# A fused attention and MLP block: two centred tiles, finer loads, new instruction orders

## The chip, the cores and the metric

The kernel runs on one core of one Trainium2 chip. The metric is the device time of one execution in microseconds (us), the median of several executions. A run is called fast when it is near the fastest of its kernel; slow ones are named. "Clock" is the clock granted to TensorE as a share of full speed.

The engines are TensorE (PE; its weight loads are PEld), VectorE (DVE), ScalarE (ACT), GpSimd (POOL) and SyncE (SP), which here only issues DMAs. A *transposing DMA* reads a tile from SBUF and writes it back transposed.

## The reference

```
phi = lambda t: where(t > 0, t + 1, exp(t)) + 1e-6        # 16 heads of 28
q, k, v = split(layernorm(x) @ wqkv)                      # x: 2048 x 448, bf16
kv  = einsum("bhsd,bhse->bhde", phi(k), v)
z   = einsum("bhsd->bhd", phi(k))
o   = einsum("bhqd,bhde->bhqe", phi(q), kv) / (phi(q) . z + 1e-6)
h   = x + o @ wo
n   = layernorm(h)
out = h + (gelu(n @ w_gate) * (n @ w_up)) @ w_down        # 448 -> 1792 -> 448
```

The 2048 rows are 16 tiles of 128. Tile t needs statistics, normalisation and a transpose before TensorE can project it to K and Q (four matmuls of 448 columns each, called K_t and Q_t below).

## The kernel before

Every instruction is a task with a name, an engine, and the buffers it reads and writes. The semaphores follow from the buffers. The order on each engine is a plain list of task numbers, found by a search outside the kernel, so an engine waits for its next task even if a later one could run:

```
ORDERS = ("26 34 32 43 41 63 66 ...", ...)                # one string per engine: PE, ACT, DVE, POOL, SP
```

Loads are issued in this order, all on SP but tile 1:

```
dma_x("sp", 0, 1);  tx1 = dma_x("act", 1, 2)
dma_w3("sp", wqk_sb, 0, 2 * D, b_wqk, "dwqk")             # Q and K weights together, 672 KB
dma_w1("sp", wqk_sb, 0, 2 * D, b_wqk, "dwqk_t")           # their last 64 rows
dma_x("sp", 2, 4); dma_x("sp", 4, 8); dma_x("sp", 8, 12); dma_x("sp", 12, 16)
# ... V weights, output weights
```

The first four tiles are normalised on DVE and transposed on PE, the others on POOL and by a transposing DMA:

```
def ln_tile(t):
    ln_stats(...)                                         # DVE: mean and variance
    ln_rstd_act(...)                                      # ACT: ln, then exp, gives 1/std
    if t < N_PE_TR:                                       # 4
        # DVE: xnn = (x - mean) * rstd                    "normD_t"
        # PE: four 128x128 transposes; ACT and DVE copy half of the result each to xnT
    else:
        # POOL: xnn = (x - mean) * rstd                   "normP_t"
        G.add("sp", lambda e: e.dma_start_transpose(xnT[:, t, :, :], xnn[:, i, :]), ...)   # "xT_t"
```

Later the same pattern returns: the attention output of tiles 2p and 2p+1 is divided by its denominator on DVE ("pn"), transposed by one DMA for the pair ("oT_p") and multiplied on PE ("the output projection of pair p"). V itself is never made: PE sums phi(K) times the normalised x over all tiles, in PSUM (the memory that TensorE writes to), and multiplies the sum by the V weights ("the fold"). TensorE first runs a warm-up of ones times ones, `WARM = 40` matmuls of 128 columns, while nothing else is there to do.

## Time and profile before

| | before |
|---|---|
| time, median of 3 | 194.24 us (194.19 to 194.25) |
| profiled execution: span, clock | 197.8 us, 0.95 (a slow execution) |
| PE, DVE, ACT, POOL busy in it | 98, 67, 39, 26% |
| second profile of the same kernel (first experiment): span, clock | 193.1 us, 1.00 |

### The profile page before, as it was taken

How to read it: one execution, taken by the hardware profiler on the slowest of the kernel's cores; microseconds unless marked ns; L12 is line 12 of the kernel's file. 1: busy time of each engine (PE TensorE's matmuls, PEld its weight loads, DVE VectorE, ACT ScalarE, POOL GpSimd, SP SyncE). 2: the span in 40 equal slices, each digit the busy share in tenths (PEclk: the TensorE clock that was granted, in tenths of full speed). 3: DMA queues.
4: the chain of work that ended last, by engine and by line, in shares of the span. 5: the costliest groups of instructions: out<-in, count | busy, mean ns of one | idle time of the engine just before them, and what ended most of it. 6: DMA issues, size and time to landing. Idle time of an engine off the chain costs nothing.

```text
span 197.8 us, 4145 instructions
## 1 busy us (share of the span) xinstructions
PE 193.7 (98%) x1572; PEld 106.9 (54%) x1572; DVE 132.0 (67%) x355; ACT 78.1 (39%) x226; POOL 50.7 (26%) x92
## 2 busy tenths in 40 slices
PE   7999999999999999999999999999999999999995
PEld 7554555555767776654454445444444454444454
DVE  3899988999999989988786537244445422444412
ACT  3797645599943324141330420023444200334200
POOL 7067710640451955235222024000000000000000
PEclk9999999999999999999999999999999999999999
DMA  6966449994587046420217272600200010100011
GB/s 194 375 174 88 94 96 209 221 215 63 102 291 124 16 50 117 102 53 23 56 26 153 57 56 52 133 21 30 46 0 3 0 46 4 46 0 3 0 46 46
DMA packets 35331, 16.97 MB, mean 86 GB/s; under 512 B 27696, under 2 KB 34032, under 8 KB 35312
## 3 DMA queue, kind: packets, MB, share of 16 engines
q1 hardware_dynamic: 35168, 16.60, 38.4%
q8 instruction: 12, 0.20, 0.4%
q10 hardware_dynamic: 144, 0.11, 0.2%
q14 instruction: 7, 0.06, 0.1%
HBM read 8.26 MB, written 1.84 MB: 51 GB/s over the span
## 4 chain that ended last, share of the span: by engine, by line
PE 90%; DMA 4%; DVE 4%; POOL 1%; issue 0%; DVEq 0%; POOLq 0%
PE ps L603 42%; PE ps L575 22%; PE ps L404 9%; PE ps L523 7%; PE ps L423 5%; PE ps L605 3%; DMA x_sb<-in_A_x_dram 2%; DVE st L348 2%; DMA xnT<-xnn 2%; DVE pk L417 1%; PE ps L471 0%; PE ps L462 0%; POOL wqk_sb L302 0%; PE ps L550 0%; DVE xnn L370 0%; DVE mv L349 0%
## 5 line engine op out<-in xcount | busy, mean ns | idle before, releaser
L605 PE MATMUL ps<-hnT,wgu_sb 64*128 64x512 bf16 (+1 forms) x490 | 89.9, 342 | 0.0
L603 PE MATMUL ps<-hnT,wgu_sb 64*128 64x512 bf16 (+1 forms) x490 | 89.6, 342 | 0.0
L623 ACT ACTIVATE gl<-ps 128x256 bf16<-128x256 f32 x112 | 37.1, 381 | 88.5 <-PE ps L605 86.4
L603 PEld LDWEIGHTS ps<-hnT,wgu_sb 64*128 64x128 bf16 x490 | 46.3, 96 | 35.1 <-issue 3.1
L625 DVE TENSOR_TENSOR hh<-ps,gl 128x256 bf16<-128x256 f32 x112 | 42.5, 416 | 34.0 <-ACT gl L623 33.7
L605 PEld LDWEIGHTS ps<-hnT,wgu_sb 64*128 64x128 bf16 x490 | 45.2, 96 | 3.7 <-DVE hh L625 0.5
L575 PE MATMUL ps<-wd_sb,hh 128*128 128x448 bf16 (+1 forms) x238 | 45.2, 351 | 0.0
L575 PEld LDWEIGHTS ps<-wd_sb,hh 128*128 128x128 bf16 x238 | 23.3, 99 | 21.1 <-issue 1.3
L404 PE MATMUL ps<-wqk_sb,xnT 128*128 128x448 bf16 x128 | 28.2, 362 | 0.1
L488 POOL TENSOR_TENSOR t<-pq,zbc 128x448 f32<-128x448 bf16 x15 | 16.6, 1115 | 33.3 <-DVE pq L484 20.5
L579 DVE TENSOR_TENSOR x_sb<-ps,x_sb 128x448 bf16<-128x448 f32 (+1 forms) x17 | 10.0, 592 | 19.6 <-PE ps L575 19.6
L348 DVE BATCH_NORM_STATS2 st<-x_sb 128x6 f32<-128x448 bf16 x32 | 19.1, 612 | 3.5 <-DMA x_sb<-in_A_x_dram 3.4
L404 PEld LDWEIGHTS ps<-wqk_sb,xnT 128*128 128x128 bf16 x128 | 12.3, 99 | 12.1 <-DMA xnT<-xnn 0.5
L423 PE MATMUL ps<-pk,xnn 128*128 128x448 bf16 x64 | 14.4, 363 | 0.0
L523 PE MATMUL ps<-w,pqnT 112*128 112x448 bf16 x64 | 14.1, 362 | 0.0
L558 POOL TENSOR_SCALAR hn<-x_sb,nm,rs 128x448 bf16<-128x448 bf16 x14 | 10.9, 779 | 8.1 <-DMA hnT<-hn 7.4
L529 DVE TENSOR_TENSOR x_sb<-ps,x_sb 128x448 bf16<-128x448 f32 x16 | 9.5, 617 | 3.8 <-PE ps L523 3.8
L415 ACT ACTIVATE e<-ps 128x448 bf16<-128x448 f32 x16 | 8.7, 541 | 5.4 <-PE ps L404 3.6
L417 DVE SCALAR_TENSOR_TENSOR pk<-ps,e 128x448 bf16<-128x448 f32 x16 | 9.9, 616 | 0.2
L388 POOL TENSOR_SCALAR xnn<-x_sb,nm,rs 128x448 bf16<-128x448 bf16 x12 | 9.0, 749 | 3.5 <-ACT rs L357 3.5
L423 PEld LDWEIGHTS ps<-pk,xnn 128*128 128x128 bf16 x64 | 6.5, 101 | 6.2
L495 DVE TENSOR_TENSOR pqn<-pq,rd 128x448 bf16<-128x448 bf16 x16 | 9.6, 622 | 0.0
(65 smaller groups left out, 125.0 us busy)
## 6 DMA issues: line engine op xcount, KB each, us to landing
out_dram<-x_sb SPq DMA_DIRECT2D x15, 112.0 KB, 1.7
wd_sb<-in_B_w_down_dram SPq DMA_DIRECT2D x1, 1568.0 KB, 7.7
x_sb<-in_A_x_dram SPq DMA_DIRECT2D x3, 448.0 KB, 5.4
wgu_sb<-in_B_w_gate_dram SPq DMA_DIRECT2D x1, 896.0 KB, 11.9
wgu_sb<-in_B_w_up_dram SPq DMA_DIRECT2D x1, 896.0 KB, 16.5
wqk_sb<-in_A_wqkv_dram SPq DMA_DIRECT2D x1, 672.0 KB, 4.8
wgu_sb<-in_B_w_gate_dram SPq DMA_DIRECT2D x1, 672.0 KB, 6.0
wgu_sb<-in_B_w_up_dram SPq DMA_DIRECT2D x1, 672.0 KB, 8.4
```

Source lines behind the costliest of these rows:

```text
L348: op("dve", lambda e: e.bn_stats(st[:, t, :], src_ap), [b_src], [b_st[t]], "bnst%s_%d" % (tag, t))
L404: ins = e.matmul(ps[:, bk, 0:D], xnT[:, t, k, :], wqk_sb[:, k, c0:c0 + D], start=(k == 0), stop=(k == 3))
L417: op("dve", lambda e: e.scalar_tensor_tensor(pk[:, ip, :], psK, EPS, e1[:, i, :], ALU.max, ALU.add), [b_ps[bk], b_e1[i]], [b_pk[ip]], "pk_ ...
L423: ins = e.matmul(ps[:, BK_PT[c], 0:D], xnn[:, t % XN_R, c * 128:(c + 1) * 128], pk[:, ip, :], start=(t == 0), stop=(t == T - 1))
L488: op(eng, lambda e, t=t, n=n: e.tensor_tensor(t1[:, n, :], pq[:, t, :], zbc[:, :], ALU.mult), [b_pq[t]] + b_z, [b_t1[n]], "t1%s_%d" % (eng ...
L523: ins = e.matmul(ps[:, BK_OUT[n], 0:D], pqnT[0:GW, i2, n, g, :], w2[:, g, :], start=(g == 0), stop=(g == NG - 1))
L558: op("pool", lambda e, t=t, sh=sh: e.tensor_scalar(hn[:, sh, 0:D], x_sb[:, t, :], nm2[:, t:t + 1], rs2[:, t:t + 1], ALU.add, ALU.mult), [b ...
L575: ins = e.matmul(psO, hh[:, j, (t % HR) * 128:(t % HR + 1) * 128], wd_sb[:, j, c0:c1], start=(j == 0), stop=(j == NJ - 1))
L603: e.matmul(psG[:, jj * N:(jj + 1) * N], wgu_sb[A_, k, j * 128:(j + 1) * 128], hnT[A_, ka_, c0:c0 + N], start=(k == 0), stop=(k == NK - 1))
L605: ins = e.matmul(psU[:, jj * N:(jj + 1) * N], wgu_sb[B_, k, j * 128:(j + 1) * 128], hnT[B_, kb_, c0:c0 + N], start=(k == 0), stop=(k == NK ...
L623: G.add("act", lambda e, gi=gi, cs_=cs_, psG=psG: e.activation(gl[:, gi, cs_], psG[:, cs_], AF.Gelu_apprx_tanh), r=[b_ps[BK_G[i]]], w=[b_g ...
L625: op("dve", lambda e, dst=dst, srcU=srcU, srcL=srcL: e.tensor_tensor(dst, srcU, srcL, ALU.mult), [b_ps[BK_U[i]], b_glh], [b_ar[j_][t % HR] ...
```

## The change

Its intent is to start the dense matmul work earlier. The first two tiles are only centred before their transpose. Since a row of (x - mean) times the weights only lacks the factor 1/std of that row, that factor is applied as the scale of the activations that read K and Q. Tile 1's statistics move to ACT. Q and K weights and x come in more pieces, K before Q. All loads stay ahead of the transposing DMAs, as before. All five orders are new, over the whole kernel.

```diff
-    WARM = 40
+    CEN = (0, 1);  ACT_ST = (1,);  WARM, WARM2, NW2 = 33, 0, 0
-    SEQ = "Q0 K0 K1 Q1 K2 Q2 ..."
+    SEQ = "K0 K1 Q0 K2 Q1 Q2 ..."
...
-        dma_w3("sp", wqk_sb, 0, 2 * D, b_wqk, "dwqk")
-        dma_w1("sp", wqk_sb, 0, 2 * D, b_wqk, "dwqk_t")
-        dma_x("sp", 2, 4)
-        dma_x("sp", 4, 8)
+        dma_w1("sp", wqk_sb, 0, 2 * D, [None, b_wqt], "dwqk_t")
+        dma_wqk(1);  dma_x("sp", 2, 3);  dma_wqk(0);  dma_x("sp", 3, 4)
+        dma_x("sp", 4, 6);  dma_x("sp", 6, 8)
...
+            if t in ACT_ST:          # sum(x)/D and sum(x*x)/D by two ACT passes with accum_out
+                act_exp(... AF.Identity, scale=1.0 / D, accum_out=mv1[:, t, 0:1] ...)
+                act_exp(... AF.Square, scale=D ** -0.5, accum_out=mv1[:, t, 1:2] ...)
...
+                if t in CEN:         # xc = x - mean
+                    op("dve", lambda e: e.tensor_scalar(xc[...], x_sb[:, t, :], mv1[:, t, 0:1], None, ALU.subtract), ...)
...
+            sc = rs1[:, t:t + 1] if t in CEN else 1.0
+            eks.append(act_exp(lambda e: e.activation(e1[:, i, :], psK, AF.Exp, scale=sc), ...))
+            if t in CEN:             # relu on ACT, then an all-SBUF add on DVE ("pka")
+                act_exp(lambda e: e.activation(pk[:, ip, :], psK, AF.Relu, scale=sc), ...)
...
 ORDERS: every number changed
```

## The prediction

> **What bounds the kernel now.** I read the page from the top: busy shares, forty slices, chain that ended last. Then the timeline of the first 24 us, TensorE's timeline up to 60 us, and the busy time by stretch.
>
> ```profile
> PE 193.7 (98%) x1572; PEld 106.9 (54%) x1572; DVE 132.0 (67%) x355; ACT 78.1 (39%) x226; POOL 50.7 (26%) x92
> ...
> PE 90%; DMA 4%; DVE 4%; POOL 1%; issue 0%; DVEq 0%; POOLq 0%
> ```
>
> TensorE (PE) is busy for 193.7 of 197.8 us, and the last chain is 90% PE. The rest of the chain lies before about 18 us: x loads, statistics, one transposing DMA. So matmul work sets the time, and a change that takes away no matmul can only start the dense part earlier or close holes in it. How much is there? The timeline, PE rows (start, length, operation, idle before):
>
> ```profile
> 1.11 4.30 PE L342 MATMUL ps<-ones_bf 128*128 128x128 bf16 x40 [1.11 <-POOL ones_bf L315]
> 5.37 0.38 PE L378 MATMUL ps<-ident,xnn 128*128 128x128 bf16 x4
> 6.07 0.40 PE L378 MATMUL ps<-ident,xnn 128*128 128x128 bf16 x4 [0.32 <-DVE xnn L370]
> 6.31 3.30 PE L404 MATMUL ps<-wqk_sb,xnT 128*128 128x448 bf16 x16
> 9.45 0.90 PE L378 MATMUL ps<-ident,xnn 128*128 128x128 bf16 x8
> 10.21 1.73 PE L404 MATMUL ps<-wqk_sb,xnT 128*128 128x448 bf16 x8
> ```
>
> The 4.3 us of ones times ones is warm-up, not work. Real projections start at 6.31. A projection's four matmuls start 0.79 us apart from the next four (11.78, 12.57), 0.197 each, so sixteen need 3.15: 6.31 to 9.45 is dense. The eight transposes start 0.055 us apart and need 0.45; they take 9.45 to 10.21, so 0.3 is lost, to the normalised tile 3 on VectorE (DVE). One hole follows:
>
> ```profile
> 17.29 0.95 PE L423 MATMUL ps<-pk,xnn 128*128 128x448 bf16 x4
> 18.30 0.96 PE L404 MATMUL ps<-wqk_sb,xnT 128*128 128x448 bf16 x4
> ```
>
> 18.30 should be 18.08: 0.2 lost, put down to a transposing DMA. From there to 60 us I find no hole, only starts at their pitch. What can be won is therefore the delay before 6.31, plus 0.3, plus 0.2.
>
> What sets 6.31? The chain of tile 0:
>
> ```profile
> 3.37 0.63 DVE L348 BATCH_NORM_STATS2 st<-x_sb 128x6 f32<-128x448 bf16 x1 [3.37 <-DMA x_sb<-in_A_x_dram]
> 4.03 0.18 DVE L349 BATCH_NORM_AGGREGATE mv<-st 128x2 f32<-128x6 f32 x1
> 4.24 0.29 ACT L355 ACTIVATE ln<-mv,eps_t 128x1 f32<-128x1 f32 x1 [1.75 <-DVE mv L349]
> 4.57 0.20 ACT L357 ACTIVATE rs<-ln 128x1 f32<-128x1 f32 x1
> 4.85 0.37 DVE L370 TENSOR_SCALAR xnn<-x_sb,mv,rs 128x448 bf16<-128x448 bf16 x1
> 5.79 0.38 ACT L383 ACTIVATE xnT<-ps 128x256 bf16<-128x256 bf16 x1 [0.28 <-PE ps L378]
> 5.92 0.28 DVE L385 COPY xnT<-ps 128x256 bf16<-128x256 bf16 x1
> ```
>
> x lands at 3.37, is normalised at 4.85, and its transpose is in SBUF at 6.20. Two other things end at nearly the same moment: tile 1's transposes, issued ahead of the first projection, at about 6.3, and the QK weights, issued at 1.24 with 4.8 us to landing by the page's list of issues: 1.24 + 4.8 = 6.04. So all three have to move together, which explains why the change is a bundle.
>
> **What the Trainium skill says.** "TensorE: Matmul & The Clock Gate", Part 1, says that the array runs at half rate until it has been busy for a free-running window of about 3.4 us, with the transition near 4 us. The trace agrees: warm-up weight loads last 152 ns and drop to 98 at about 5.1, 4.0 after 1.11. "DMA: Bandwidth & Descriptors", "Anatomy of one DMA", says that the fixed cost of a transfer is mostly the write receipt; in this trace a 112 KB piece of x takes 2.6 us, one of twice the size 4.3 behind the weights, so what is queued ahead counts as much as size. "ScalarE: Activation LUTs", "What ACT_TABLE_LOAD costs", says that a per-partition operand in place of an immediate adds about 93 ns to an activation. Rows with such a bias (0.29) and without (0.20) agree. "VectorE: DVE Perf Modes", "Why PSUM operands drop a tier", says that a PSUM operand costs a perf mode; here the PSUM combine takes 0.616 and an all-SBUF bf16 add 0.381.
>
> **The change part by part.**
> *Centring.* Tiles 0 and 1 are transposed as x minus mean; 1/std is applied per row as the scale of the activations that read K and Q. That is exact, since rows of x become rows of the product. Off tile 0's path: from 4.21 (mean ready) to 4.85, 0.6 us. Centring starts at 4.25, ends at 4.62; the path from 4.85 to 6.20 took 1.35, so the same steps end at 5.60.
> *Statistics of tile 1 on ScalarE (ACT).* Two passes of 448 (I take 0.54, as L432; an estimate, from SBUF) from 3.5 to 4.6 replace 0.63 + 0.18 on DVE. But ACT also evicts half of tile 0: after these passes come tile 0's ln (0.29) and exp (0.20) and tile 1's ln (0.29), so that eviction starts at about 5.4 and ends near 5.8. So the first projection starts at about 5.85, not 5.65.
> *Weights.* Ahead of K now stand x0, x1, the 112 KB tail and K itself, 0.67 MB, in place of about 1.0 MB. Bytes by time (busy time by stretch: 221 GB/s in 2 to 3 us, 335, 405) reach 0.67 MB at about 4.3; today's 1.0 MB is reached at 5.1 and lands at 6.04, 0.9 later. So K lands near 5.2 to 5.6, in time for 5.85. Q, 0.45 MB later, lands near 6.5 and is wanted at 5.85 + 8 x 0.197 = 7.4: hidden. x2 should land near 5.5 and x3 near 6.7, where both landed at 6.74.
> *Warm-up.* 33 matmuls instead of 40 at 0.107 us: it ends near 4.65, when the first transposes can come. It costs nothing if the clock still rises at about 5.1.
> *Work added and moved.* ACT: two statistics passes and two relus of K, some 2 us, less nothing. DVE: one bn pair (0.8) and two PSUM combines (1.2) go, two adds (0.76) and two small memsets come; about 1 us less. POOL: two more normalisations (1.4) and two memsets fewer (1.3).
> *Tiles 2 and 3.* The orders are plain lists of numbers that I decoded by counting operations in the diff. PE runs K0, K1, Q0, transposes of 2, Q1, transposes of 3, K2. Twelve matmuls from 5.85 end at 8.2, Q1 near 9.2. Tile 2's statistics start after the evictions, at 5.9, and it is normalised near 7.6: in time. Tile 3's rsqrt stands in ACT's order after K0's relu and exp, K1's exp, two ln and an eviction: about 9.2, and its DVE normalisation ends near 9.7. So transposes of tile 3 wait about 0.5, and K2 starts near 9.9 to 10.0 instead of 10.21.
>
> Sum: 0.46 earlier at the start, 0.2 more lost at tile 3 (0.5 against 0.3), 0.2 gained if the hole at 18.3 closes, as the transposing DMAs start some 1.3 us earlier. Net 0.46 - 0.2 + 0.2, about **0.45 us**. The ceiling, with no hole at all, is 0.46 + 0.3 + 0.2, about 1.0. The timed runs may have larger holes than this profile: they last 194.24, the profiled execution 199.48 at a granted clock of 0.95. At a higher clock the matmuls shrink, and the DVE, busy 14.9 of 15 us from 10 to 25, begins to bind; there its relief of about 1 us would be worth more. I choose 0.7.
>
> **Rivals.**
> *Another wait takes the place (order-bound).* ACT becomes the gate: it was busy 4.94 of 5 us from 10 to 15 and gets 2 us more, mostly before 10. If tile 3's rsqrt slips another 0.5, all is given back: 194.2 to 194.5. The two sums on ACT may also need a separate step to read the accumulator, which the trace cannot show. Against it: DVE relief, and an order searched for this.
> *The K weights stay the gate.* Rows of 896 bytes instead of 1792 mean more packets for the same bytes; if K still lands at 6.0 the start gains 0.25 and the total is 194.0. For it: today's landing is only 0.3 before the start.
> *The clock rises late.* With 33 matmuls and thin transposes from 4.7 to 5.9, the window in which the array counts as busy may be missed; the next is 3.4 us away, in which half rate would cost up to 1.7: 195.3. I give it one in ten. Against it: 3.5 us of warm-up are left, and the switch at 5.1 fell in before the old first transpose.
> *All hidden anyway.* DVE bounds the stretch from 10 to 25 us, not PE, so an earlier start ends at the same place: 194.2. Against it: PE is dense there at its own pitch.
>
> **Range and chances.** 194.24 - 0.7 = **193.5 us**. Low end: the whole ceiling and half a us of holes that only timed runs have, 192.7. High end: start gained and given back, 194.4. Two per cent would be 3.9 us, four times the ceiling in this trace: faster 0.02. Slower by 3.9 would need a late clock and a new stall together: 0.02. Within 2%: 0.96.
>
> **What would show it.** In the changed kernel's timeline: centring at 4.25; first projection between 5.6 and 6.0, a K projection not Q; K weights 3.5 to 4 us from issue to landing; tile 2's statistics before 6; tile 3's transposes apart from tile 2's with a wait of about 0.5 before them, ended by DVE and behind it ACT; K2 near 9.95; no hole near 18; from 25 us on the same rows as before, all earlier by one constant. The prediction is wrong if the first projections run 0.37 apart instead of 0.197 (clock), if the start stays at 6.2 (weights), or if the reordered middle between 30 and 60 us shows holes that were not there.

## The result, and the profile after

The changed kernel took **194.82 us** (194.72, 194.83, 194.81, 193.74, 195.02, and one slow run of 196.75 at clock 0.991). The kernel before, on the same chip in the same rounds, took 194.25 (194.16 to 194.46). The ratio is 1.0018, 95% interval 0.9994 to 1.0043. Ratios here and below are the mean time of one kernel's fast runs over that of the other's fast runs of the same rounds, so not quite the ratio of the medians quoted. The time is within 2%, as predicted, but outside the range: 194.82 against a high end of 194.4.

The page of the changed kernel, its busy line and its last chain:

```profile
PE 186.8 (97%) x1565; PEld 110.0 (57%) x1565; DVE 130.7 (68%) x355; ACT 79.3 (41%) x232; POOL 52.4 (27%) x96
...
PE 88%; DMA 6%; DVE 2%; SPq 2%; issue 0%; ACT 0%; DVEq 0%; ACTq 0%
```

DMA has gone from 4 to 6% of the chain. The chain in order of time says where one piece of that is (start, length, what):

```profile
59.63 0.39 ACT gl L667
60.06 4.84 DMA pqnT<-pqn
64.95 1.69 PE ps L567 x8
```

At 65 us, where the prediction saw only matmuls at their pitch, TensorE waits for a transposing DMA that takes 4.84 us. The timeline of the beginning, PE rows of the changed kernel (start, length, operation, idle before):

```profile
1.04 3.70 PE L357 MATMUL ps<-ones_bf 128*128 128x128 bf16 x33 [1.04 <-POOL eps_t L331]
4.57 1.02 PE L412 MATMUL ps<-ident,xc 128*128 128x128 bf16 x8
5.82 2.49 PE L439 MATMUL ps<-wqk_sb,xnT 128*128 128x448 bf16 x12 [0.23 <-DMA wqk_sb<-in_A_wqkv_dram]
8.31 0.28 PE L412 MATMUL ps<-ident,xnn 128*128 128x128 bf16 x2
8.62 0.93 PE L439 MATMUL ps<-wqk_sb,xnT 128*128 128x448 bf16 x4
9.38 0.28 PE L412 MATMUL ps<-ident,xnn 128*128 128x128 bf16 x2
10.77 0.40 PE L412 MATMUL ps<-ident,xnn 128*128 128x128 bf16 x4 [1.11 <-DVE xnn L404]
11.01 0.54 PE L439 MATMUL ps<-wqk_sb,xnT 128*128 128x448 bf16 x2
11.87 2.07 PE L439 MATMUL ps<-wqk_sb,xnT 128*128 128x448 bf16 x10 [0.33 <-DVE xnT L419]
```

The first projection (line 439) starts at 5.82, as planned. Then come two holes: 1.11 us before tile 3's transposes, ended by DVE's normalised tile, and 0.33 us inside K2, ended by DVE's copy of tile 2's second half. The same rows of the kernel before, at full clock:

```profile
6.39 3.19 PE L404 MATMUL ps<-wqk_sb,xnT 128*128 128x448 bf16 x16
9.41 0.39 PE L378 MATMUL ps<-ident,xnn 128*128 128x128 bf16 x4
10.09 0.40 PE L378 MATMUL ps<-ident,xnn 128*128 128x128 bf16 x4 [0.29 <-DVE xnn L370]
10.32 1.68 PE L404 MATMUL ps<-wqk_sb,xnT 128*128 128x448 bf16 x8
```

So the changed kernel is 0.57 us ahead at the first projection and 0.69 behind at K2 (11.01 against 10.32). Why DVE is late there is in its own rows of the changed kernel:

```profile
8.63 0.63 DVE L367 BATCH_NORM_STATS2 st<-x_sb 128x6 f32<-128x448 bf16 x1 [0.38 <-DMA x_sb<-in_A_x_dram]
...
10.35 0.36 DVE L404 TENSOR_SCALAR xnn<-x_sb,mv,rs 128x448 bf16<-128x448 bf16 x1
11.00 0.63 DVE L367 BATCH_NORM_STATS2 st<-x_sb 128x6 f32<-128x448 bf16 x1 [0.28 <-DMA x_sb<-in_A_x_dram]
11.54 0.27 DVE L419 COPY xnT<-ps 128x256 bf16<-128x256 bf16 x1
```

The copy of tile 2's second half (11.54), which K2 needs, stands in DVE's order behind statistics of tile 8 (11.00), which waited for x. Tile 3's normalisation (10.35) is held by ACT, whose rows before it are these:

```profile
7.42 0.62 ACT L454 ACTIVATE pk<-ps,rs 128x448 bf16<-128x448 f32 x1
7.94 1.15 ACT L452 ACTIVATE e<-ps,rs 128x448 bf16<-128x448 f32 x2
9.37 0.48 ACT L374 ACTIVATE ln<-mv,eps_t 128x1 f32<-128x1 f32 x2 [0.28 <-DVE mv L368]
9.76 0.36 ACT L417 ACTIVATE xnT<-ps 128x256 bf16<-128x256 bf16 x1
10.03 0.28 ACT L376 ACTIVATE rs<-ln 128x1 f32<-128x1 f32 x2
```

Tile 3's 1/std is made at 10.03. The two `ln` before it are those of tiles 3 and 5 and waited for DVE, whose statistics of tile 5 waited for x until 8.63.

Starts of some matmul groups, read from the two traces at full clock:

| | before | changed | changed minus before |
|---|---|---|---|
| first projection | 6.39 | 5.82 | -0.57 |
| K2 | 10.32 | 11.01 | +0.69 |
| the fold of K and V (all tiles' K done) | 38.61 | 39.14 | +0.53 |
| last tile group's last down projection | 185.16 | 184.97 | -0.19 |
| span | 193.1 | 192.9 | -0.2 |

One profiled execution each cannot show the 0.57 us between the medians, for executions of one kernel differ by one microsecond and more. But it shows the shape: the front loses 1.1 us against its start, and the later part, with its new orders, is shorter by 0.7 in spite of the stall at 65 us. The size of the front's loss differs from execution to execution: this one of the kernel before took 194.83, 0.6 over its median, with a stall of its own at 15.91 (below), and in a_mid, whose first 50 us are those of the changed kernel, the fold starts at 38.38.

### The profile page after: what moved, and what is told of

It is laid out like the page before. It is cut to its first block, busy times and chain, and to the rows that moved or that the text cites. A ratio compares the mean times of both kernels' runs of the same rounds, so it can differ in the third digit from the quotient of the medians.

```text
span 192.9 us, 4146 instructions
## 1 busy us (share of the span) xinstructions
PE 186.8 (97%) x1565; PEld 110.0 (57%) x1565; DVE 130.7 (68%) x355; ACT 79.3 (41%) x232; POOL 52.4 (27%) x96
## 3 DMA queue, kind: packets, MB, share of 16 engines
HBM read 8.26 MB, written 1.84 MB: 52 GB/s over the span
## 4 chain that ended last, share of the span: by engine, by line
PE 88%; DMA 6%; DVE 2%; SPq 2%; issue 0%; ACT 0%; DVEq 0%; ACTq 0%
PE ps L647 35%; PE ps L619 22%; PE ps L439 10%; PE ps L649 7%; PE ps L567 7%; PE ps L465 6%; DMA x_sb<-in_A_x_dram 3%; DMA pqnT<-pqn 3%; SPq L290 2%; DVE st L367 1%; PE ps L515 0%; DVE pk L456 0%; PE ps L506 0%; PE ps L594 0%; PE ps L548 0%
## 5 line engine op out<-in xcount | busy, mean ns | idle before, releaser
L649 PE MATMUL ps<-hnT,wgu_sb 64*128 64x512 bf16 (+1 forms) x490 | 86.2, 334 | 0.0
L647 PE MATMUL ps<-hnT,wgu_sb 64*128 64x512 bf16 (+1 forms) x490 | 86.0, 333 | 0.0
L669 DVE TENSOR_TENSOR hh<-ps,gl 128x256 bf16<-128x256 f32 x112 | 42.7, 419 | 32.5 <-ACT gl L667 32.2
L647 PEld LDWEIGHTS ps<-hnT,wgu_sb 64*128 64x128 bf16 x490 | 45.5, 94 | 24.9 <-issue 2.2
L649 PEld LDWEIGHTS ps<-hnT,wgu_sb 64*128 64x128 bf16 x490 | 42.5, 94 | 5.7 <-DVE hh L669 3.3
L619 PE MATMUL ps<-wd_sb,hh 128*128 128x448 bf16 (+1 forms) x238 | 43.4, 341 | 0.0
L439 PE MATMUL ps<-wqk_sb,xnT 128*128 128x448 bf16 x128 | 27.2, 353 | 0.6 <-DVE xnT L419 0.3
L465 PE MATMUL ps<-pk,xnn 128*128 128x448 bf16 x64 | 13.8, 353 | 0.1
L422 POOL TENSOR_SCALAR xnn<-x_sb,nm,rs 128x448 bf16<-128x448 bf16 x14 | 10.4, 749 | 4.0 <-ACT rs L376 3.8
L371 POOL TENSOR_SCALAR nm<-mv 128x1 f32<-128x1 f32 (+1 forms) x21 | 4.8, 236 | 24.0 <-DVE mv L368 23.4
L452 ACT ACTIVATE e<-ps 128x448 bf16<-128x448 f32 x14 | 7.6, 546 | 6.9 <-PE ps L439 5.4
L567 PEld LDWEIGHTS ps<-w,pqnT 112*128 112x128 bf16 x64 | 5.6, 98 | 7.5 <-DMA pqnT<-pqn 1.1
```

The lines of the kernel that those rows point to most:

```text
L422: op("pool", lambda e: e.tensor_scalar(xnn[:, i, 0:D], x_sb[:, t, :], nm1[:, t:t + 1], rs1[:, t:t + 1], ALU.add, ALU.mult), [b_x[t], b_nm1 ...
L439: ins = e.matmul(ps[:, bk, 0:D], xnT[:, t, k, :], wqk_sb[:, k, c0:c0 + D], start=(k == 0), stop=(k == 3))
L465: ins = e.matmul(ps[:, BK_PT[c], 0:D], xnn[:, t % XN_R, c * 128:(c + 1) * 128], pk[:, ip, :], start=(t == 0), stop=(t == T - 1))
L567: ins = e.matmul(ps[:, BK_OUT[n], 0:D], pqnT[0:GW, i2, n, g, :], w2[:, g, :], start=(g == 0), stop=(g == NG - 1))
L619: ins = e.matmul(psO, hh[:, j, (t % HR) * 128:(t % HR + 1) * 128], wd_sb[:, j, c0:c1], start=(j == 0), stop=(j == NJ - 1))
L647: e.matmul(psG[:, jj * N:(jj + 1) * N], wgu_sb[A_, k, j * 128:(j + 1) * 128], hnT[A_, ka_, c0:c0 + N], start=(k == 0), stop=(k == NK - 1))
```

## The experiments

Fifteen runs, all correct: the kernel before again, and fourteen edited kernels. The first two calls ran on one chip, the third and the fourth on two others, so kernels of different calls are best compared by their ratios to before. Medians leave out slow runs; the changed kernel's is over all six (194.81 without the slow one). "Before" in each line is the kernel before in the same rounds. Where a line says stall, it is the start-to-start distance of two matmuls less their normal pitch (columns at 2.4 per nanosecond plus 2.5 ns), read from the records of the trace; it is a little longer than the idle time that a page row shows.

| experiment | us, median (range) | ratio to before, 95% |
|---|---|---|
| changed kernel | 194.82 (193.74 to 195.02) | 1.0018 (0.9994 to 1.0043) |
| a_front: tile 3 first | 196.0 (195.41 to 196.46) | 1.0090 (1.0072 to 1.0108) |
| a_load: loads as before | 194.95 (194.2 to 195.93) | 1.0039 (1.0013 to 1.0065) |
| a_mid: orders of before from 50 us on | 195.35 (194.2 to 195.89), one slow 199.18 left out | 1.0047 (1.0018 to 1.0077) |
| a_delay: 10 more warm-up matmuls | 196.77 (195.14 to 197.18) | 1.0094 (1.0056 to 1.0131) |
| a_oT: pair 3's row repaired | 194.16 (193.11 to 194.73) | 0.9973 (0.9941 to 1.0006) |
| a_front2: tile 3 first, ACT too | 197.65 (196.26 to 199.19) | 1.0165 (1.0112 to 1.0218) |
| b_late: front of before, repaired late orders | 193.78 (193.47 to 194.4) | 0.9968 (0.9943 to 0.9993) |
| a_shift: warm-up of fewer instructions | 193.27 (192.75 to 194.19) | 0.9948 (0.9920 to 0.9976) |
| a_swap68: tiles 6 and 8 swapped | 194.06 (193.72 to 195.51) | 0.9992 (0.9962 to 1.0023) |
| a_best: swap and repair | 194.03 (193.25 to 194.91) | 0.9977 (0.9943 to 1.0011) |
| b_late_shift | 193.94 (193.71 to 194.56) | 0.9978 (0.9956 to 1.0001) |
| **a_swap_shift: swap and fewer instructions** | **193.0 (192.72 to 193.58)** | **0.9928 (0.9905 to 0.9951)** |
| a_all: swap, repair, fewer instructions | 193.33 (192.9 to 193.41), one slow 280.58 left out | 0.9938 (0.9916 to 0.9959) |
| b_shift: before with fewer instructions | 194.5 (193.74 to 195.0) | 1.0001 (0.9976 to 1.0025) |

### First call: front, loads, late orders

**b_again** is the kernel before without an edit, for a profile at full clock.

> The kernel before once more, for a profile at the full clock, since its first profile fell in a slow execution at a granted clock of 0.95. The dense matmul part of the changed kernel, 5.82 to 190.6 us less its stalls of some 3.5, is about 181.3 us. If the kernel before, at full clock, starts its projections at 6.3 and ends near 190.1, it must have some 2.5 us of stalls of its own that the slow profile (0.5 us in the first 20 us) did not show: I expect 2 to 3 us of stalls, or else a granted clock below 1.0 in its ordinary runs.

It took 194.83 in its one execution, at clock 1.00, and is the comparison used above. Its stalls after the first projection add up to 2.4 us, as expected. One thing in it corrects my reading: the fold starts at 38.61 where the slow profile had 38.76, although the clock was 1.00 against 0.95. Were this stretch made of matmuls at their pitch, it would have been some 1.3 us shorter (32.5 us from first projection to fold, times 1 - 0.189/0.197, the starts of matmuls in the two profiles). The difference is nearly all one hole: K4 waits 1.04 us at 15.91 here, while in the slow profile it starts at its pitch (14.93). So "PE is dense there at its own pitch" was true of one slow profile and not of this one. What makes the hole comes with b_shift.

**a_front** puts tile 3's statistics and normalisation, and tile 2's second half of transposes ("tr1_2"), ahead of other work:

```diff
 PE:  ... q_0 tr0_2
-q_1 tr1_2
+tr1_2 q_1
 DVE: ... normD_2
-bnst_5 bnag_3 bnag_5 ck_0 bnst_4 ck_1 bnag_4 normD_3 bnst_8 evxD_2
+bnag_3 ck_0 evxD_2 normD_3 bnst_5 bnag_5 bnst_4 bnag_4 evxD_3 ck_1
 ACT: ... rk_0 ek_0
-ek_1 ln_3 ln_5 evxA_2 rs_3 rs_5 rk_1 ln_4 eq_0
+ln_3 rs_3 evxA_2 ek_1 ln_5 rs_5 evxA_3 rk_1 ln_4 eq_0
```

> The changed kernel with only the orders of the first 12 us altered: tile 3's aggregate, rsqrt and normalise, and tile 2's evictions, go ahead of the statistics of tiles 5, 4 and 8 that wait for late x pieces. Theory ORDER (the in-order VectorE queue puts work that waits for late x pieces ahead of tile 3): the waits of 1.28 us and 0.49 us before tile 3's transposes and K2 fall to under 0.4 together, and the time falls by 1.2 to 1.6 us, to about 193.2. Theory LOADS (the loads as a whole end too late, 15.3 us, and the transposing DMAs land behind them at 15.8): the same waits vanish but come back before K5 at 14 to 16 us; the time falls by at most 0.4, to 194.3.

K2 started at 9.98, close to what I had predicted for the change. It did not help: the bill moved. PE rows of this run:

```profile
9.98 0.92 PE L439 MATMUL ps<-wqk_sb,xnT 128*128 128x448 bf16 x4
11.86 0.93 PE L439 MATMUL ps<-wqk_sb,xnT 128*128 128x448 bf16 x4 [0.96 <-ACT pk L454]
13.36 0.93 PE L439 MATMUL ps<-wqk_sb,xnT 128*128 128x448 bf16 x4 [0.57 <-ACT pq L476]
```

After K2 the next projection waits 0.96 us for ACT's relu of K1 to free its PSUM bank, and the one after that 0.57 us for ACT again. By K4 the 1.03 us gained at K2 are gone (17.16 against 17.10 in the changed kernel). So in this stretch ACT has no room: what is done sooner for tile 3 is done later for the tiles before. That the kernel took 196.0, over a microsecond more than the changed one, has another reason in its trace: K6 waits 1.09 us, at 20.51, for a transposing DMA of 3.86 us. What slows such DMAs is found further down.

**a_load** gives the changed kernel the load list of before (Q and K weights whole, x in pieces of 1, 1, 2, 4, 4, 4 tiles):

```diff
-dwqk_t dwk dx2 dwq dx3 dx4 dx6 dx8 ...
+dwqk dwqk_t dx2 dx4 dx8 ...
```

> The changed kernel with only the loads of before: Q and K weights in one transfer ahead of their tail, x in pieces of 2 and 4 tiles. First projection near 6.1 instead of 5.82. Theory LOADS: tiles 4 to 7 land near 7.9 and 8 to 11 near 9.0 instead of 8.6 and 11.0, so statistics 5 and 8 no longer hold tile 3; stalls before K2 fall from 1.8 to about 0.6; all loads end near 12.7 instead of 15.3; time 193.6 to 193.9. Theory ORDER alone: the order of ScalarE and VectorE keeps tile 3 late whatever lands; time 194.5 or more.

The first projection started at 6.19, just after the weights landed (6.15), and K2 at 11.73, both later than in the changed kernel. In the traces with the finer loads and the short warm-up the first projection starts between 5.77 and 6.14, so the finer loads bring it forward by 0.05 to 0.4 us. The time, 194.95, is within the spread of the changed kernel's, and the fold starts only 0.10 later (39.24). That is not because K2 does not matter: this trace lacks two breaks after K2 (0.49 and 0.28 us) that the changed kernel's has. In all eight traces with the changed kernel's TensorE order that have no such break (this one, a_mid, a_delay, a_oT, a_shift, a_swap68, a_best, a_swap_shift), K4 starts 5.57 or 5.58 us after K2, so what is lost at K2 is lost.

**a_mid** keeps the changed kernel to about 50 us and takes the old orders from there.

> The changed kernel up to about 50 us, then the orders of before on every engine (and the warm-up pow of GpSimd ahead of the first products with z instead of among them). The stall of 0.99 us at 64.95 before the third output projection should vanish if the new orders of the second half caused it: time down by 0.7 to 1.0, to about 193.7. If instead it comes from matmuls being faster at full clock than the engines that feed them, the old orders stall there as well and the time stays at 194.6.

The stall at 65 us was gone from its trace and still it took 195.35. Going back to the old late orders is no repair.

### Second call: the start itself, the stall, the late orders alone

**a_delay** runs the warm-up longer:

```diff
-    WARM, WARM2, NW2 = 33, 0, 0
+    WARM, WARM2, NW2 = 43, 0, 0
```

> The changed kernel with 43 warm-up matmuls instead of 33, nothing else: it takes the early start away again, the first projection moves from about 5.9 to about 6.4 us. Theory START (the prediction's: the first projection sets when the dense part ends): the time rises by 0.4 to 0.6 us over the changed kernel. Rival (the start is not on the path; K2 waits for tile 3 behind late x pieces and ScalarE, whatever the start): it rises by 0.15 or less. A late rise of the clock would show as first projections 0.37 us apart in the short warm-up and not here.

The first projection came at 6.59, 0.77 later, but K2 at 11.12, only 0.11 later: the start is off the path. Yet it took 196.77, two us more (1.5 by the ratios). The trace has three stalls on transposing DMAs: 1.39 us before K6, 1.12 at 56.6 and 1.10 at 67.0. Ten more warm-up matmuls did something to DMAs 50 us later. That was the clue for the third call.

**a_oT** repairs what I took for the cause of the stall at 65 us. In POOL's order a power (0.58 us) and the denominators of tile 7 stood ahead of those of tile 6, which is wanted first:

```diff
 POOL: mhalf t1p_1 ... t1p_5
-t1p_7 powwarm t1p_6
+t1p_6 t1p_7          # powwarm right after mhalf
 DVE:  dr_6 rd_6 pn_6 moved ahead;  ACT: deA_6 moved ahead
```

> The changed kernel with one local repair in the middle: the warm-up pow of GpSimd and the product for tile 7 no longer stand ahead of the product for tile 6, and tile 6's reduction, reciprocal and normalisation go earlier on VectorE and ScalarE, so that the transposing DMA for tiles 6 and 7 is issued near 57.5 us instead of 60.06. Expected: the wait of 0.99 us before the third output projection vanishes (under 0.15) and, the rest being TensorE at its pitch, the time falls by 0.8 to 1.0, to about 193.7. If the earlier reductions hold up the products of the gate, small new waits of 0.2 to 0.4 us appear near 56 us.

The DMA of pair 3 was issued at 58.33 in place of 60.06 and landed at 62.04. The stall was gone and the time was 194.16. In its trace another stall of 1.75 us stands before K6, so that the profiled run, at 194.73, gained nothing.

**a_front2** is a second try at the front with ACT's relu of K1 and its exp and relu of Q0 moved ahead too.

> A second try at the order of the first 15 us in the changed kernel: tile 3 and tile 2's evictions ahead of later statistics as in the first try, but the activations that free the banks of K1 and Q0 come early too, and the first product of K with x stands ahead of K3. Theory ORDER: K2 near 10 and no wait over 0.4 until Q3, which ends near 14.5; the time falls by 0.7 or more, to under 194. Theory LOADS: the same start of K2, but K5 waits until about 15.7, since the first transposing DMA lands behind the loads; the time falls by 0.4 or less.

It was the slowest: 197.65. Three runs at clock 1.00 took 196.26 to 196.64, three at 0.990 or 0.991 took 198.65 to 199.19. K2 came at 9.46, but Q3 then waited 1.84 us for ACT, so this hand order lost too. The profiled run is one of the slow ones: in it, after the stall of 2.64 us before K6, the matmuls from 23.5 to 26 us ran at half pitch.

**b_late** has the front of the kernel before and, from 50 us on, the repaired orders of the change.

> The kernel before up to about 50 us, then the orders of the changed kernel with the repair of the third output projection. The changed orders go 14 times between gate-and-up matmuls and others, those of before 18 times; from the first gate matmul to the end the changed kernel took 141.4 us in its profile with a stall of 0.99 in it, the kernel before 141.9. So I expect the second half alone to be worth 1.2 to 1.4 us once repaired: 192.9 to 193.1 against 194.2. If the saving is of another source than the orders (the chip, the clock), the time stays at 194.

It took 193.78, ratio 0.9968, with an interval (to 0.9993) that just excludes 1. So the late orders, once repaired, give a small gain without any of the front's edits. Its trace still has a stall of 1.24 us before K4, on a transposing DMA of 4.10 us.

### Between the calls: what the slow transposing DMAs have in common

A transposing DMA here normally takes 2.5 us (a tile of x), 2.9 (a tile of the normalised h, before the MLP) or 3.1 (a pair), but in each trace a few take 4 to 5. The records of single DMA packets gave the answer. Besides the data, the page lists a queue "q8 instruction: 12, 0.20, 0.4%". These are twelve packets of 16384 bytes, on average some 250 TensorE instructions apart. In fifteen traces (all but the slow profiles of the kernel before and of a_all; the clock was full, 0.991 in a_front2) there are 435 transposing DMAs issued after 17 us. **All 25 that took over 4.5 us had such a packet start between issue and landing**, and so had 57 of the 60 over 4.0; the other three were issued less than 0.5 us after one. Put the other way, of the 97 with a packet 57 took over 4.0, of the 338 without one 3. A packet that started in a DMA's last half microsecond did no harm, for instance at 20.13 in one that landed at 20.37 after 2.51 us. Before 17 us, while loads still land, a transposing DMA can be slow without a packet: the changed kernel's first two took 4.51 and 3.65 us, and its first packet came at 20.13.

The Trainium skill, "Runtime: NRT & Kernel Launch", section "Instruction fetch mechanics", says that an engine's instruction memory is refilled in blocks of 16 KiB, 256 instructions, by DMA, at a cost "mostly hidden". The trace agrees on the size and, on average, on the spacing. For TensorE itself the cost is hidden too: in these traces no stall over 0.4 us follows within 3 us of a packet that met no transposing DMA. The transposing DMA beside it is what pays. The skill's "DMA: Bandwidth & Descriptors", "Queues, rings and completion order", says that each DMA engine serves its queues in turn, whole packets at a time. These packets last 0.9 to 1.6 us, one of them 2.0, so this would fit a delay of 1.2 to 1.9. The records do not say on which DMA engine a packet ran, so this is the likely mechanism and not one that is shown.

In the changed kernel the DMA views of two stretches show it. First 60 to 65 us of the changed kernel (queue lines and issue lines; the last number is the time to landing):

```profile
q1 hardware_dynamic: 2078, 0.52, 85.4%
q8 instruction: 1, 0.02, 1.1%
...
pqnT<-pqn SPq DMA_TRANSPOSE x1, 4.8
```

One instruction packet is in the window, at 62.83 by its record, and the pair's DMA takes 4.8 us. That packet may be moved without touching any order: if the packets follow the count of TensorE instructions, a warm-up that does the same columns in fewer of them shifts all later packets.

### Third call: move the packets

**a_shift** is the changed kernel with this edit only:

```diff
-                for _ in range(n):
-                    ins = e.matmul(ps[:, 3, 0:128], ones_bf[:], ones_bf[:], start=True, stop=True)
+                for _ in range(n // 4):      # 8 matmuls of 512 columns
+                    ins = e.matmul(ps[:, 3, 0:512].rearrange("p (a b) -> p a b", a=4), ones_bf[:],
+                                   ones_bf[:].unsqueeze(1).to_broadcast([128, 4, 128]), start=True, stop=True)
+                for _ in range(n % 4):       # and one of 128
+                    ins = e.matmul(ps[:, 3, 0:128], ones_bf[:], ones_bf[:], start=True, stop=True)
```

> The changed kernel with its warm-up done by 8 matmuls of 512 columns and one of 128 in place of 33 of 128: the same columns, so the same length, but 24 matmuls (with their weight loads some 48 TensorE instructions) fewer; no order and no load is touched. In every trace so far 16384-byte instruction packets come one per some 250 TensorE instructions, and the transposing DMAs that have one in flight take 4 to 5 us in place of 2.5 to 3.1. Fetch theory: the packet of 62.8 us comes some 1.5 us later, at about 64.3, after the transposing DMA for the third output projection has landed (issued 60.1, landing 63.2 in place of 64.9); the stall of 0.99 us before that projection goes with no change of order. Order theory (the DMA is issued 2.6 us later than in the kernel before, and that is all): landing and stall stay as they were, 64.9 and 0.99. Time: fetch theory 194.0 or below, unless the first packet, moved as well, now holds up tile 6's transpose; order theory 194.8.

The ten more warm-up matmuls of a_delay were the other direction of the same thing: there packets at 54.45 and 64.88 met the DMAs of pairs 2 and 3. Here the packet moved to 64.18 and the DMA, issued at 60.43, landed at 63.65. The DMA view of 60.4 to 63.7 us of this run has no instruction queue at all:

```profile
q1 hardware_dynamic: 1624, 0.41, 64.3%
...
pqnT<-pqn SPq DMA_TRANSPOSE x1, 3.2
```

In both runs two more transposing DMAs follow the pair's by 1.34 and 2.79 us, so these are not what slowed it. The stall went with no change of order, and the time fell to 193.27: by the ratios to before 0.7%, some 1.4 us, under the changed kernel, with an interval that excludes 1. The order theory, which I had held through the second call, falls as the whole cause. The late issue took away the slack and the packet did the rest: in the kernel before the pair is issued at 57.47, early enough to cover even a slow DMA, and in a_oT the earlier issue got it out of the packet's way.

**a_swap68** lets tiles 6 and 8 change places in statistics, normalisation and transposing DMAs, since PE wants tile 6 first:

```diff
-SP:  xT_5 xT_4 xT_8 xT_6 xT_7 ...       DVE: normD_3 bnst_8 evxD_2 ...
+SP:  xT_5 xT_4 xT_6 xT_8 xT_7 ...       DVE: normD_3 bnst_6 evxD_2 ...
```

> The changed kernel with tiles 6 and 8 changing places in the statistics, the normalisation and the transposing DMAs on all four engines; TensorE's order stays. Theory (late x, and the fourth transposing DMA as tight as can be): VectorE's eviction of tile 2's second half no longer stands behind the statistics of tile 8, which waited for x to 10.98, so the 0.49 us inside K2 goes to about 0.1, and tile 6's transposing DMA is the third and lands 1.2 us earlier, so that the stall of 1.4 to 2.6 us before K6, seen in three of the variants, cannot come. Time 194.2, and a narrower spread than the 194.7 to 195.0 of the changed kernel. Rival (these waits are covered by slack later on): 194.8 as before.

K2 ran without the break (twelve matmuls in a row from 10.78) and the fold started at 38.38, 0.76 earlier than in the changed kernel. The swap is not shown to be the cause: a_mid, without it, has no break either and its fold at 38.38 too. In both traces x of tiles 8 to 11 had landed by 10.21, in the changed kernel's at 10.98. The time was 194.06, ratio 0.9992, not separable from the changed kernel's 1.0018. The stall at the third output projection was there again (1.11 us; DMA from 59.30 to 64.25, packet at 62.25).

**a_best** has both the swap and the repair.

> Tiles 6 and 8 swapped and the third output projection's row repaired (both edits together), as a candidate that beats both kernels. If the two gains add: 0.6 for the repair (194.16 against 194.8) and 0.5 for the swap, so 193.4 to 193.7, ratio to the kernel before about 0.995. If the swap is covered by slack: 194.1.

It took 194.03: the gains did not add. Its first packet, at 17.88, met tile 7's transposing DMA (4.18 us) and cost 1.26 us before K7. The swap frees tile 6 and leaves tile 7 to be hit.

**b_late_shift** is b_late with the same warm-up of fewer instructions.

> The kernel before up to 50 us and the changed kernel's repaired orders from there (193.78, the fastest so far), with its warm-up done by 10 matmuls of 512 columns in place of 40 of 128: some 60 TensorE instructions fewer. Fetch theory: the first instruction packet moves from 13.1 to about 16, off the first transposing DMA (which then takes 2.5 us in place of 4.1) and on to the third or fourth; the stall of 1.24 us before K4 goes, at most 0.3 comes before K6. Time 193.0 to 193.4. Rival (that first DMA is slow because the loads are still landing, and the packet is a bystander): the stall stays, 193.8.

The stall before K4 went, as expected. But the first packet came at 24.85, not near 16, met other transposing DMAs of x, and a stall of 0.91 us came at 28.05 in its place. The time, 193.94, is the same as b_late's. Moving packets is no gain by itself; it depends on what they hit.

### Fourth call: controls and the combination

**a_swap_shift** has the swap and the warm-up of fewer instructions.

> The changed kernel with the warm-up of fewer instructions and with tiles 6 and 8 swapped, the orders of its later part untouched. If the two losses are separate (K6's stall by the first instruction packet, the third output projection's by the fourth), both are gone in every run: 192.8 median with a spread under 1 us; if the swap does nothing beside the moved packets, 193.3 as without it. No stall above 0.3 us after 12 us.

It is the fastest kernel of all and beats both: **193.0 us**, ratio 0.9928 to before, with a spread of 0.86 us. Whether the swap adds to a_shift's 193.27 is not settled, for their intervals overlap. Its PE rows after 10 us:

```profile
10.77 0.40 PE L415 MATMUL ps<-ident,xnn 128*128 128x128 bf16 x4 [0.84 <-DVE xnn L407]
11.00 2.58 PE L442 MATMUL ps<-wqk_sb,xnT 128*128 128x448 bf16 x12
13.42 1.68 PE L468 MATMUL ps<-pk,xnn 128*128 128x448 bf16 x8
```

The wait for tile 3 is still there, and after it no stall over 0.15 us to the end. The pair's DMA took 3.20 us.

**a_all** adds the repair to that.

> The same with the third output projection's repair as well. Packet theory: nothing is left for the repair to gain, so 192.8 again, within 0.3 of the run without the repair. Order theory (late issue costs by itself): 0.5 better than without the repair, 192.3.

Five fast runs gave 193.33, not better than 193.0. So once no packet meets that DMA the repair is worth nothing, which is what the packet theory said. Its profiled run was an outlier at clock 0.659 (280.58 us), so there is no trace of it to read.

**b_shift** is the control: the kernel before, with the warm-up of fewer instructions alone.

> The kernel before with the warm-up of fewer instructions alone (10 matmuls of 512 columns in place of 40 of 128). If the gain of 1.5 us in the changed kernel came of the warm-up itself (a clock that rises earlier, say), it comes here too: 193.0. If it came of where the packets fall among its transposing DMAs, here there is little to gain: the first packet leaves the first to third transposing DMA, where it costs 0.2 to 1.0, and the others meet DMAs with slack: 193.8 to 194.3.

It took 194.5, ratio 1.0001. The new warm-up has no gain of its own. Its trace shows the exchange. K4 starts at 14.95 without a stall, and later:

```profile
28.02 2.24 PE L407 MATMUL ps<-wqk_sb,xnT 128*128 128x448 bf16 x11 [0.80 <-DVE eq L486]
```

The DMA view of 23.8 to 27.9 us of the same run says why:

```profile
q8 instruction: 1, 0.02, 2.0%
...
xnT<-xnn SPq DMA_TRANSPOSE x3, 4.1
```

The releaser in brackets is the wait that came last by the profile, and it misleads here. The same happened in the second profile of before, where K4 is put down to ACT:

```profile
15.91 0.92 PE L404 MATMUL ps<-wqk_sb,xnT 128*128 128x448 bf16 x4 [0.88 <-ACT pq L432]
```

That ACT instruction ran at 15.39 there and at 15.48 in b_shift, where K4 nevertheless started at 14.95. What differs is tile 4's transposing DMA: 11.88 to 15.77 there, with a packet at 12.89, and 11.96 to 14.48 in b_shift, without one.

## Why the prediction was wrong, point by point

- **The earlier start** was right: 0.57 us (0.46 predicted), first projection 5.82 (5.85), a K projection, centring at 4.09 (4.25). Over all traces it starts at 5.77 to 6.14 with the finer loads and the short warm-up, at 6.31 to 6.55 with the front of before. The K weights landed at 5.78, just outside 5.2 to 5.6, and were the gate by 0.23 us; in five traces (0.23 to 0.67 us) they were, so the rival "the K weights stay the gate" was in part true.
- **"Transposes of tile 3 wait about 0.5, and K2 starts near 9.9 to 10.0" is the step that failed in the front.** The idle time was 1.11, K2 started at 11.01, and 0.33 us more were idle inside K2. The walk followed ACT's order to put tile 3's 1/std at "about 9.2"; it was made at 10.03. It left out DVE's order, in which the statistics of tile 5 stand ahead of tile 3's aggregate. In all nine traces at full clock with this order (changed, a_mid, a_load, a_delay, a_oT, a_shift, a_swap68, a_best, a_swap_shift) K2 starts 2.37 or 2.38 us after these statistics do, and a_front, which moves them behind tile 3's normalisation, has K2 at 9.98. These statistics start at 8.17 to 9.61; they waited for x over 0.3 us in two of the traces only (changed, 0.38, and a_shift, 0.48), so late x adds to the loss and the order makes it. At the fold the prediction had booked 0.45 us gained; the trace has 0.53 lost, and that is the greater part of the miss. Smaller terms, not tested one by one: the activations that read K and Q with a per-row scale take 0.62 us against 0.54 without, and the two statistics passes are each followed by a reading of the accumulator. I had named the last as a doubt and booked nothing for it.

```profile
3.93 0.19 ACT L387 ACTIVATION_READ_ACCUMULATOR e<-x_sb 128x1 f32 x1
```

- **The rival "Another wait takes the place (order-bound)"** described what happened in the front: start gained, then given back. The gate was DVE's order first (ACT itself waited 0.28 us for it at 9.37) and ACT behind it: two orders by hand, a_front and a_front2, moved the wait to ACT and did not remove it. a_delay shows it from the other side: a start 0.77 us later moves K2 by 0.11.
- **"No hole near 18"** held in the profiled run, but not as a property of the kernel. In four variants that share its order of transposing DMAs (a_front, a_front2, a_delay, a_oT) K6 waits 1.1 to 2.6 us for the fourth one, which met a packet.
- **"From 25 us on the same rows as before, all earlier by one constant" failed outright.** I decoded the first 12 us of the new orders and took the rest as unchanged. From the fold to the last down projection the changed kernel takes 145.83 us and before 146.55. In these traces the late orders are worth more than the whole front: with the stall moved away it is 144.93 (a_shift, 39.51 to 184.44), 1.6 us less than before. About 1.0 of it can be named in the records: 14 in place of 18 changes between gate/up matmuls and others, at about 0.1 us each, and waits of 0.38, 0.26 and 0.13 gone, less two new changes of 0.1. The rest was not traced.
- **The term that the sum did not have** is the stall before the third output projection. The prediction named new holes in the reordered middle, between 30 and 60 us, as a sign of being wrong, but gave them no cost; this one came at 65. It is 0.97 to 1.11 us in the traces of all six kernels with these late orders unrepaired and the warm-up of 128 columns, and absent in all those that repaired the row or moved the packet and left a readable trace. With it the changed kernel takes 194.82, with only its packets moved 193.27, which would have been inside the range of 192.7 to 194.4 and close to 193.5. But that would have been right for a wrong reason: in its trace the fold starts at 39.51, 0.90 later than before, and all of the gain comes after it. The number itself also leaned on a guess: the sum was 0.45, and 0.7 was chosen.
- **Smaller readings that were off.** x of tile 2 landed at 6.08 and of tile 3 at 7.24 (5.5 and 6.7 expected), so tile 2's statistics started at 6.11, not before 6. Tile 0 only begins to be normalised at 4.85; the path of 1.35 from there is right. On TensorE the second half of tile 2's transposes stands behind Q1, not ahead of it.
- **"The clock rises late"** did not happen as feared. In the changed kernel's profile the eight transposes ran at half pitch (0.107 us) until 5.3 and the projections at full pitch from 6.1 on. In several variants the first two or three projection matmuls still ran at half pitch, about 0.3 us in all.
- **DVE's relief** is real: from 3 to 39 us, by the busy time by stretch at full clock, DVE works 30.79 us in place of 32.84, 2 us less where I had counted about 1. But ACT works 24.38 in place of 23.20, and tile 3 waited for both.

What stays open: why the first packet comes at 16.4 us in one trace and at 20.1 in another of the same TensorE order, and at 24.85 where 16 was expected (b_late_shift), which would explain part of the spread from run to run; and on which DMA engine it meets the transposing DMA. That the timed runs, which leave no trace, lose as the profiled ones do is inferred from the medians moving with the edits.

## What to carry to other kernels

When a change brings new orders for the whole kernel, compare the orders to the end before pricing its headline; the part that nobody announced was worth more here than the part that gave the change its name. A transposing DMA on a tight schedule needs about 2 us of slack beyond its usual time, or a check of where the instruction packets fall: twenty-four instructions with their weight loads taken from a warm-up gave some 1.4 us, and in another kernel nothing. And the engine that the profile names as releaser is only the last one seen; another run in which the same instruction is just as late and nobody waits settles it.

## What the Trainium skill lacked or had wrong

- "Runtime: NRT & Kernel Launch" calls the cost of an instruction block "mostly hidden". It is for the fetching engine, but a transposing DMA that has one in flight takes, in 57 of 97 cases, 4 to 5 us in place of 2.5 to 3.1, and up to 1.8 us of that showed as a TensorE stall before K6 at full clock (a_oT), 2.6 in a_front2; no page has this.
- "DMA: Bandwidth & Descriptors" gives bandwidths for transposing DMAs and no time from issue to landing for one of a single tile: here 2.5 us for 128 x 512 bf16 and 3.1 for a pair of output tiles, when nothing meets it.
- "ScalarE: Activation LUTs" says that an activation can give an accumulator output, and not that reading it is an instruction of its own (no page says so for ScalarE): 0.19 us after each of the two passes.
